# Two layers of linear attention and MLP, twice: passes, steps and small operations in another order

## The chip, the cores and the metric

The kernel runs on one core of a Trainium2 chip. The metric is the device time of one execution in microseconds (us); the time before is the median of three runs. A core has TensorE (PE in the profile, with PEld for its weight loads), VectorE (DVE), ScalarE (ACT), GpSimd (POOL) and SyncE (SP), each with its own queue of instructions that is worked in order. They wait for one another by semaphores. DMAs are issued from a queue and run beside the engines. Matrix products land in PSUM, which has eight banks of 128 x 512 f32 values; the other tiles lie in SBUF.

## The reference

x is 2048 rows of 512 values in bf16. Four layers follow one another, attention and MLP in turn, with the same weights in both rounds:

```
x = x + A(layernorm(x));  x = x + B(layernorm(x));  x = x + A(layernorm(x));  x = x + B(layernorm(x))
A: q, k, v = x @ wqkv, 32 heads of 16;  phi(t) = where(t > 0, t + 1, exp(t)) + 1e-6
   kv = sum over rows of phi(k) x v;  z = sum over rows of phi(k)
   out = (phi(q) @ kv) / (phi(q) . z + 1e-6), heads joined, @ wo
B: relu(x @ w1) @ w2, with w1 512 x 1376 and w2 1376 x 512
```

The layernorm subtracts the mean of a row's 512 values and divides by the root of their variance plus 1e-5. There is no softmax: attention is linear, so the sums over all rows (kv and z) must be complete before any output row can be made.

## The kernel before

The 2048 rows are 16 tiles of 128 rows, in four chunks of four tiles. All weights stay in SBUF; x stays there too, as `xin` (bf16) and `xres` (f32, the running sum).

The program is a graph of operations in Python (`g.add`, `add_flex`). Each names its engine, what it reads and writes by keys such as `("ps", b)` or `("big", unit)`, and a duration in ns (the constants `C_...` at the top). `_list_schedule` (from line 114) then simulates the machine: it repeatedly takes the operation that can start first, among the next `WINDOW` ones of each engine in the order in which they were added, gives PSUM tiles one of eight banks, lets an operation with alternatives (`add_flex`) choose its engine, and so writes down a fixed order for every engine's queue. `TAIL` is what it adds for a result to be seen. Semaphore waits are worked out from that order. So the order of `g.add` calls is only a priority, and a change in a cost, a key or a place can move instructions of the whole kernel.

The attention layer has these parts. `a_k` (four matmuls a tile) makes a tile's k; `phi_evac` takes it out of PSUM: ScalarE writes t + 1 (line 506) and exp(t) (508), VectorE clips the exp (510) and takes the larger (516). `a_q` does so for q, four groups of four matmuls a chunk. `a_z` sums phi(k) over rows with a column of ones. The value projection is not made for each row: `a_g` makes G = (normalised x)^T phi(k) in four PSUM banks, `a_g_evac` copies it, `a_kv` multiplies it with the v weights, and `a_m` masks the result to heads (line 582) and multiplies it with wo, giving `Mf` (589). `a_den` makes the denominators (matmuls with 32 columns), their log and its negative exp; `a_pqs` spreads the reciprocals over rows with 32-row matmuls (`Esel`) and scales phi(q) on VectorE (619). `a_fin` is four matmuls a tile of scaled phi(q) with Mf. `resid` (531 and 534) adds the result to x and sums each row; ScalarE's Square (540) sums the squares.

The MLP layer has `b_h` (ten column groups of 128, four chunks) with `b_relu` (641 and 642), `b_hl` for the last 96 columns in groups of 32, and `b_group` for the second product: for each of four groups of tiles, first the 32-row passes with the last 96 rows of w2 (`mk_small`, twelve matmuls that open four PSUM banks, or five in the very last group), then ten matmuls a tile for the other rows. A group `il` takes tile `il` of every chunk, so it needs the relu of all chunks.

The norm of a chunk, `ln_chunk`, is a chain of small operations on 128 x 4 values: mean, minus its square, variance, variance plus epsilon on VectorE (451, 453, 455, 457), the power -0.5 on GpSimd (459), and -mean times that (`nbias`) on VectorE (461). `ln_norm` then normalises a tile on ScalarE (470), VectorE (472) or GpSimd (475). The tiles are transposed by PE (494, evacuated by 498 or 499) for the first chunk or two of the first layer and for the first chunk of MLP layers, and by DMA (480) elsewhere. In the first layer the statistics come from `bn_stats` (439, 440) on VectorE; `ln_first(0)` treats tile 0 alone (708 to 714) and tiles 1 to 3 together.

All loads go out on SP's queue: tile 0 of x, tiles 1 to 3, the K weights, the Q weights, the other chunks of x, the V weights and the rest (lines 376 to 391). Sixteen matmuls on zeros (`WARM`, line 407) run while x is on its way. `layer_steps` gives the steps of a layer with what each needs; the loop behind it weaves the steps of the next layer in as soon as their chunk is there. In attention, `bar` is what follows the last k tile: z, denominators, G, kv, Mf and the last chunk of q; `p2(t)` is fin, norm and transposes of one chunk.

Of the kernel before, what the change touches and what calls it, by code (L numbers as in the profile page):

```python
# [31 lines left out]
C_POOL_POW = 1000.0  # L32
C_POOL_NORM = 900.0
C_SP_ISSUE = 60.0
TAIL = {PE: 70.0, ACT: 230.0, DVE: 80.0, POOL: 300.0, SP: 0.0}
SYNC_LAT = 40.0
LN_EXP_SET = 6
WINDOW = {PE: 64, ACT: 80, DVE: 80, POOL: 12, SP: 6}


class _Op:
    __slots__ = ("eng", "emit", "reads", "writes", "dur", "lat", "sdeps", "odeps", "idx",
                 "seq", "dma", "name", "t_start", "t_done", "issued", "pos", "nsucc", "alts")
# [19 lines left out]
class _Graph:  # L63

    def __init__(self):
        self.ops = []
        self.last_w = {}
        self.readers = {}
        self.tile_ops = {}
        self.ntiles = 0  # L70

# [5 lines left out]
    def add(self, eng, emit, reads=(), writes=(), dur=100.0, lat=0.0, dma=False, name=""):  # L77
        op = _Op(eng, emit, tuple(reads), tuple(writes), dur, lat, dma, name)
        op.idx = len(self.ops)
        deps = {}  # L80
# [36 lines left out]
def _list_schedule(ops, tile_ops, vbank, nbanks=8):  # L117
# [15 lines left out]
    pend = {e: [o for o in ops if e in engs_of(o)] for e in ENGINES}  # L133
# [4 lines left out]
    remaining = len(ops)  # L138

    def ready_time(o):  # L140
# [10 lines left out]
        if need:  # L151
            fr = sorted(x for x in bank_free if x is not None)
            if len(fr) < len(need):
                return None
# [5 lines left out]
    while remaining:  # L160
        best = None
        for e in ENGINES:
# [33 lines left out]
            if cand is not None and (best is None or cand[0] < best[0] - 1e-9  # L196
                                     or (abs(cand[0] - best[0]) <= 1e-9 and cand[1].idx < best[1].idx)):
# [46 lines left out]
def build_kernel(nc, A_x, A_wqkv, A_wo, B_w1, B_w2, out, n_layers_pairs=2, K_STT=0, Q_STT=0, A_PE_CHUNKS=1, windows=None,  # L244
                 WARM=16, SPLIT0=True, TAIL_SPLIT=True, LAST_HALVES=True, FIRST_PE_CHUNKS=2,
# [22 lines left out]
    with es:  # L268
# [32 lines left out]
        nm2 = sb("nm2", [128, NT], F32)  # L301
        var = sb("var", [128, NT], F32)
# [6 lines left out]
        veps0 = sb("veps0", [128, 1], F32)  # L309
        rstd0 = sb("rstd0", [128, 1], F32)  # L310
        nbias0 = sb("nbias0", [128, 1], F32)
# [28 lines left out]
        def dma(emit, reads, writes, xfer_ns, name):  # L340
# [5 lines left out]
            op = g.add(SP, _emit, reads, writes, dur=C_SP_ISSUE, lat=xfer_ns, dma=True, name=name)  # L346
# [23 lines left out]
        def h_keys(c):  # L370
            return [("big", il * RU + c) for il in range(4)]
# [3 lines left out]
        def ld_x(t, lo=0):  # L375
            dma(lambda e, t=t: e.dma_start(xin[:, 4 * t + lo:4 * t + 4, :], x_v[:, 4 * t + lo:4 * t + 4, :]),
                [], [("xin", i) for i in range(4 * t + lo, 4 * t + 4)], 1500.0 * (4 - lo) / 4.0, "ld_x%d" % t)
        dma(lambda e: e.dma_start(xin[:, 0, :], x_v[:, 0, :]), [], [("xin", 0)], 450.0, "ld_x0a")
# [4 lines left out]
        for t in range(1, NCH):  # L383
            ld_x(t)
# [590 lines left out]
```

## Time and profile before

| what | us |
|---|---|
| median of 3 runs (lowest, highest) | 293.84 (293.66, 294.12) |
| the profiled execution, its own time | 294.0 |
| its span in the profile | 292.3 |
| PE busy | 283.3 (97%) |
| DVE busy | 153.4 (52%) |
| ACT busy | 172.5 (59%) |
| POOL busy | 31.8 (11%) |
| first matmul on zeros; first on x (a transpose) | 1.23; 7.04 |
| first K product; first fin; first product of the MLP | 8.13; 59.16; 75.02 |
| first fin of the third layer; its MLP | 198.27; 214.13 |
| last matmul ends | 289.67 |

Busy is the sum of an engine's instructions, and the page's forty slices give its share of each fortieth of the span (7.3 us) in tenths. Matmuls overlap in the array, so their recorded lengths (380 ns for 512 columns) are longer than the distance between two starts; rates are read from starts. Some matmul records are missing. An engine that idles costs nothing unless another waits for it.

### The profile page before, as it was taken

The page shows a single profiled execution, that of the slowest core. Times are in us where ns is not written, and L with a number is a line of the kernel's source. Part 1 is how long each engine was busy: PE and PEld are TensorE (multiplying, and loading weights), DVE is VectorE, ACT ScalarE, POOL GpSimd, SP SyncE. Part 2 cuts the span into 40 slices and gives each one's busy share as a digit, 9 for nine tenths or more (in the row PEclk, how much of TensorE's full clock was granted, in tenths as well). Part 3 has the DMA queues.
Part 4 walks back from the last instruction along what each step waited for, and adds up shares of the span by engine and source line. Part 5 has one row for each costly group of instructions (what it writes and reads, how often), then busy time and mean ns, then how long its engine had stood idle before and what let it go on. Part 6 is the DMA issues. An engine that isn't in the chain of part 4 may idle for free.

```text
span 292.3 us, 4292 instructions
## 1 busy us (share of the span) xinstructions
PE 283.3 (97%) x1649; PEld 128.7 (44%) x1670; DVE 153.4 (52%) x438; ACT 172.5 (59%) x354; POOL 31.8 (11%) x42
## 2 busy tenths in 40 slices
PE   7899999999999999999999999999999999999996
PEld 3354444334444444444444443444444444444443
DVE  5899774999940000347464758928994000022223
ACT  2998596687866664335644899258786766300000
POOL 3102100002430000022020300000243000000000
PEclk9999999999999999999999999999999999999999
DMA  7995320000370000030303400000038000001222
GB/s 222 357 374 107 63 27 0 2 0 0 72 147 0 0 2 0 3 72 11 61 2 72 72 3 0 2 0 0 3 64 152 1 2 0 2 9 63 72 74 72
DMA packets 33780, 15.97 MB, mean 55 GB/s; under 512 B 25312, under 2 KB 33248, under 8 KB 33760
## 3 DMA queue, kind: packets, MB, share of 16 engines
q1 hardware_dynamic: 33760, 15.70, 21.8%
q8 instruction: 13, 0.21, 0.3%
q14 instruction: 7, 0.06, 0.1%
HBM read 7.31 MB, written 2.10 MB: 32 GB/s over the span
## 4 chain that ended last, share of the span: by engine, by line
PE 88%; DVE 6%; DMA 2%; ACT 2%; issue 1%; SPq 1%
PE ps L523 87%; DMA xin<-in_A_x_dram 2%; DVE big L619 2%; DVE xn L472 1%; DVE xres L534 1%; ACT Mf L589 1%; ACT big L506 1%; PE ps L494 0%; DVE bst L439 0%; DVE big L516 0%; DVE emscr L510 0%; ACT sqscr L540 0%; SPq L382 0%; ACT escr L508 0%; SPq L381 0%
## 5 line engine op out<-in xcount | busy, mean ns | idle before, releaser
L523 PE MATMUL ps<-Tb,w 128*128 128x512 bf16 (+1 forms) x416 | 75.0, 379 | 0.0
L523 PE MATMUL ps<-w,big 128*128 128x512 bf16 (+1 forms) x321 | 69.2, 372 | 1.3 <-issue 1.3
L641 ACT ACTIVATE big<-ps 128x512 bf16<-128x512 f32 x78 | 46.5, 596 | 19.6 <-PE ps L523 19.6
L523 PEld LDWEIGHTS ps<-Tb,w 128*128 128x128 bf16 (+1 forms) x416 | 33.5, 97 | 41.2 <-ACT big L641 1.7
L523 PEld LDWEIGHTS ps<-w,big 128*128 128x128 bf16 x330 | 31.4, 98 | 37.6 <-issue 2.3
L534 DVE SCALAR_TENSOR_TENSOR xres<-ps,xres 128x512 f32<-128x512 f32 x32 | 21.8, 687 | 47.2 <-PE ps L523 46.9
L540 ACT ACTIVATE sqscr<-xres 128x512 bf16<-128x512 f32 x48 | 29.9, 629 | 27.5 <-DVE xres L534 27.3
L506 ACT ACTIVATE big<-ps 128x512 bf16<-128x512 f32 x64 | 40.9, 643 | 7.6 <-PE ps L523 7.3
L508 ACT ACTIVATE escr<-ps 128x512 bf16<-128x512 f32 x64 | 41.3, 661 | 0.4 <-DVE emscr L510 0.4
L531 DVE TENSOR_TENSOR xin<-ps,xres 128x512 bf16<-128x512 f32 x15 | 10.4, 692 | 54.5 <-PE ps L523 54.5
L459 POOL TENSOR_TENSOR rstd<-veps,nhalf 128x4 f32<-128x4 f32 x15 | 16.1, 1072 | 175.9 <-DVE veps L457 155.8
L523 PE MATMUL ps<-Tb,wqkv 128*128 128x512 bf16 x128 | 30.6, 379 | 0.0
L523 PE MATMUL ps<-wqkv,Tb 128*128 128x512 bf16 x124 | 28.8, 379 | 1.5 <-ACT Tb L498 1.1
L523 PE MATMUL ps<-Mf,big 128*128 128x512 bf16 x126 | 28.9, 380 | 1.1 <-ACT Mf L589 0.8
L523 PE MATMUL ps<-big,xn 128*128 128x512 bf16 x124 | 29.7, 379 | 0.3
L516 DVE TENSOR_TENSOR big<-big,emscr 128x512 bf16<-128x512 bf16 x64 | 26.5, 422 | 1.2
L510 DVE TENSOR_SCALAR emscr<-escr 128x512 bf16<-128x512 bf16 x64 | 18.5, 296 | 12.3 <-ACT escr L508 12.1
L619 DVE TENSOR_TENSOR big<-big,ps 128x512 bf16<-128x512 bf16 x32 | 19.9, 680 | 1.3 <-PE ps L523 1.3
L523 PEld LDWEIGHTS ps<-wqkv,Tb 128*128 128x128 bf16 x128 | 12.1, 98 | 16.0 <-ACT Tb L498 1.5
L523 PEld LDWEIGHTS ps<-Mf,big 128*128 128x128 bf16 x128 | 11.9, 98 | 16.2 <-ACT Mf L589 1.3
L523 PEld LDWEIGHTS ps<-big,xn 128*128 128x128 bf16 x128 | 11.5, 97 | 13.1 <-issue 1.5
L523 PEld LDWEIGHTS ps<-Tb,wqkv 128*128 128x128 bf16 x128 | 11.5, 97 | 12.3 <-DVE big L619 0.4
(71 smaller groups left out, 184.6 us busy)
## 6 DMA issues: line engine op xcount, KB each, us to landing
wqkv<-in_A_wqkv_dram SPq DMA_DIRECT2D x3, 512.0 KB, 6.1
xin<-in_A_x_dram SPq DMA_DIRECT2D x3, 512.0 KB, 8.0
out_dram<-xin SPq DMA_DIRECT2D x3, 512.0 KB, 2.9
w<-in_B_w_dram SPq DMA_DIRECT2D x1, 1376.0 KB, 11.0
w<-in_B_w_dram SPq DMA_DIRECT2D x1, 1280.0 KB, 13.7
wo<-in_A_wo_dram SPq DMA_DIRECT2D x1, 512.0 KB, 8.8
xin<-in_A_x_dram SPq DMA_DIRECT2D x1, 384.0 KB, 3.3
w2l<-in_B_w_dram SPq DMA_DIRECT2D x4, 96.0 KB, 7.6
```

The costliest lines, as they stand in the source:

```text
L459: g.add(POOL, lambda e: e.tensor_tensor(rstd[:, sl], veps[:, sl], nhalf[:, 0:4], ALU.pow), [("veps", t), ("nhalf",)], [("rstd", t)], C_POO ...
L472: (DVE, lambda e: e.tensor_scalar(xn[:, i, :], src, rstd[:, i:i + 1], nbias[:, i:i + 1], ALU.mult, ALU.add), C_DVE_NORM_BF if first else 4 ...
L506: g.add(ACT, lambda e: e.activation(dst_ap, psv[:, b, :], ACTF.Identity, bias=1.0 + 1e-6, scale=1.0), [("ps", b)], [dst_key], C_ACT_PSUM, ...
L508: g.add(ACT, lambda e: e.activation(escr[:, s, :], psv[:, b, :], ACTF.Exp), [("ps", b)], [("escr", s)], C_ACT_EXP, name=name + "_exp")
L510: g.add(DVE, lambda e: e.tensor_scalar(emscr[:, s, :], escr[:, s, :], 1.0, 1e-6, ALU.min, ALU.add), [("escr", s)], [("emscr", s)], C_DVE_B ...
L516: g.add(DVE, lambda e: e.tensor_tensor(dst_ap, dst_ap, emscr[:, s, :], ALU.max), [dst_key, ("emscr", s)], [dst_key], 340.0, name=name + "_ ...
L523: last = e.matmul(o, l, r, start=st, stop=sp, skip_group_check=skip)
L531: g.add(DVE, lambda e: e.tensor_tensor(xin[:, i, :], psv[:, b, :], src, ALU.add), [("ps", b), skey], [("xin", i)], C_DVE_PSUM, name="resid ...
L534: g.add(DVE, lambda e: e.scalar_tensor_tensor(xres[:, i, :], psv[:, b, :], 0.0, src, ALU.add, ALU.add, accum_out=s1[:, si:si + 1]), [("ps" ...
L540: g.add(ACT, lambda e: e.activation(sqscr[:, q, :], xres[:, i, :], ACTF.Square, accum_out=s2[:, si:si + 1]), [("xres", i)], [("sqscr", q), ...
L619: g.add(DVE, lambda e, j=j, u=u: e.tensor_tensor(unit_ap(u), unit_ap(u), psv[:, bs[j], :], ALU.mult), [("ps", bs[j]), ("big", u)], [("big" ...
L641: g.add_flex([(ACT, lambda e: e.activation(h_evac_ap(c, t), pin(), ACTF.Relu), C_ACT_PSUM), (DVE, lambda e: e.tensor_scalar(h_evac_ap(c, t ...
```

## The change

- *32-row passes.* `b_group` is split into `b_small` (the 32-row passes of a group) and `b_main` (its other matmuls, for some of its tiles). The passes of group il + 1 are put between the third and the fourth tile of group il, and those of group 0 ahead of the last column group of the last `b_h`. The keys of the hidden values are kept for each chunk (`("big", unit, t)`) instead of for all.
- *Attention steps.* `bar` has another order: each chunk's denominator, spread and scaling stand between the parts of G; q of chunk 2 (first layer) or of chunks 0 to 2 (third layer) moves into it. Chunk 0's fin is written with Mf's part j outermost, as sixteen single matmuls into four banks (`a_fin4`). The last chunk's denominator moves from `bar` to `p2(0)`.
- *Ranks.* Operations of engines other than PE can carry an urgency (`g.urg`), which moves them forward in the scheduler's list by so many places: 300 for KVT and Mf, 100 for G's copies, 40 and 60 for chunk 0's second part and the last q. An operation that opens PSUM banks out of turn must leave one free (`RESERVE`).
- *Norm.* All the small steps of `ln_chunk` go to GpSimd, one more than before as the variance is taken in two; the norm of tiles 0 and 1 of a chunk runs on VectorE from mean and rstd, that of tiles 2 and 3 on VectorE or ScalarE; none on GpSimd.
- *First tiles.* Each of tiles 0 to 3 has its own chain with Ln and Exp on ScalarE in place of the power; later statistics wait for tile 3's norm; in the later chunks of the first layer tiles 0 to 2 are normalised on VectorE and tile 3 on ScalarE. The K weights are loaded from ScalarE's queue, x in pieces of 1, 1, 2 and 4 tiles ahead of the Q weights; `WARM` goes from 16 to 12.
- *Costs.* GpSimd's power is costed by its columns, its small steps at 150 ns, its tail at 60 ns instead of 300.

```diff
-C_POOL_POW = 1000.0
-C_POOL_NORM = 900.0
+C_POOL_POW0 = 420.0
+C_POOL_POW1 = 145.0
+C_POOL_SMALL = 150.0
...
+TAIL = {PE: 70.0, ACT: 230.0, DVE: 80.0, POOL: 60.0, SP: 0.0}
...
+RESERVE = 1
...
+        op.urg = self.urg if eng != PE else 0
...
+    def rank(o):
+        return o.idx - o.urg
+    ranked = sorted(ops, key=rank)
...
+            if o is not hd and len(fr) < len(need) + min(RESERVE, len(alloc_of[hd.idx])):
                 return None
...
         ld_x(0, 1)
-        dma(lambda e: e.dma_start(wqkv[:, :, D:2 * D], wq_v[:, :, D:2 * D]), [], [("wk",)], 1500.0, "ld_wk")
-        dma(lambda e: e.dma_start(wqkv[:, :, 0:D], wq_v[:, :, 0:D]), [], [("wq",)], 1500.0, "ld_wq")
-        for t in range(1, NCH):
-            ld_x(t)
+        ld_qk(D, "wk", ACT)
+        ld_x(1, 2)
+        ld_x(2, 4)
+        ld_x(4, 8)
+        ld_qk(0, "wq")
+        for t in range(2, NCH):
+            ld_x(4 * t, 4 * t + 4)
...
+            g.add(DVE, lambda e: e.bn_stats(bst[:, i, :], xin[:, i, :]), [("xin", i)] + ([("xn", 3)] if i > 3 else []),
+                  [("bst", i)], C_DVE_BNST, name="bnst%d" % i)
...
+        def ln_rstd_act(i):
+            g.add(ACT, lambda e: e.activation(veps[:, i:i + 1], mv[:, i, 1:2], ACTF.Ln, bias=EPS, scale=1.0),
+                  [("var", i)], [("veps", i)], 200.0, name="lnv%d" % i)
+            g.add(ACT, lambda e: e.activation(rstd[:, i:i + 1], veps[:, i:i + 1], ACTF.Exp, scale=-0.5),
+                  [("veps", i)], [("rstd", i)], 200.0, name="rstd%d" % i)
...
+            g.add(POOL, lambda e: e.tensor_scalar(mean[:, sl], s1[:, sl], -INV_D, None, ALU.mult),
+            g.add(POOL, lambda e: e.tensor_tensor(nm2[:, sl], mean[:, sl], mean[:, sl], ALU.mult),
+            g.add(POOL, lambda e: e.tensor_scalar(ex2[:, sl], s2[:, sl], INV_D, None, ALU.mult),
+            g.add(POOL, lambda e: e.tensor_tensor(var[:, sl], ex2[:, sl], nm2[:, sl], ALU.subtract),
+            g.add(POOL, lambda e: e.tensor_scalar(veps[:, sl], var[:, sl], 0.0, EPS, ALU.max, ALU.add),
             g.add(POOL, lambda e: e.tensor_tensor(rstd[:, sl], veps[:, sl], nhalf[:, 0:4], ALU.pow),
+            g.add(POOL, lambda e: e.tensor_tensor(nbias[:, sl], mean[:, sl], rstd[:, sl], ALU.mult),
...
+        def a_fin4(t, first_layer):
+            bs = [alloc_bank() for _ in range(4)]
+            for j in range(4):
+                u = pq_unit(j, t)
+                for il in range(4):
+                    mm_group(lambda j=j, il=il, u=u: [(psv[:, bs[il], :], big[:, u * 512 + 128 * il:u * 512 + 128 * il + 128], Mf[:, j, :],
+                                                       j == 0, j == 3, True)],
+                             bk(u) + [("Mf", j)], [("ps", bs[il])], C_MM512, "fin%d_%d" % (4 * t + il, j))
...
                 def o_step(il):
-                    b_group(il, last_layer)
+                    b_main(il, last_layer, 0, 3)
+                    if il < 3:
+                        b_small(il + 1, last_layer)
+                    b_main(il, last_layer, 3, 4)
...
+                def up_last():
+                    b_h(NCH - 1, range(NFULL - 1))
+                    b_small(0, last_layer)
+                    b_h(NCH - 1, range(NFULL - 1, NFULL))
```

The first layer's `bar` after the change:

```
                    if first_layer:
                        a_den(0)
                        g_rest(0)
                        a_den(1)
                        a_pqs(0)
                        g_rest(1)
                        a_kv(0, KB)
                        a_q(2)
                        a_pqs(1)
                        a_kv(1, KB)
                        g_rest(2)
                        a_den(2)
...
                    g_rest(3)
                    a_kv(2, KB)
                    a_pqs(2)
                    a_kv(3, KB)
                    a_m(KB)
                    g.urg = URG3
                    a_q(3)
                    g.urg = 0
```

## The prediction

> **What bounds the kernel now.** I read the page's busy lines and its forty slices first, then TensorE's list of waits, then the start in the timeline, and last the timeline of TensorE alone, looking for holes.
>
> ```profile
> PE 283.3 (97%) x1649; PEld 128.7 (44%) x1670; DVE 153.4 (52%) x438; ACT 172.5 (59%) x354; POOL 31.8 (11%) x42
> PE   7899999999999999999999999999999999999996
> DVE  5899774999940000347464758928994000022223
> ACT  2998596687866664335644899258786766300000
> ```
>
> TensorE (PE) is full from the third slice on at full clock. Everything else is a supplier. The change removes no matrix work, so it can only win holes in PE. These are the waits:
>
> ```profile
> PE ps L523 <- issue: 1.3, 8, 0.2
> PE ps L407 <- DVE wrm L400: 1.2, 1, 1.2
> PE ps L523 <- ACT Tb L498: 1.1, 2, 0.6
> PE ps L523 <- ACT Mf L589: 0.8, 1, 0.8
> PE ps L523 <- DVE big L516: 0.4, 1, 0.4
> ```
>
> Eight holes of "issue" (1.3 us in all) stand behind the 32-row passes; one waits for the evacuation of Mf, one for VectorE's phi, and the rest lie at the start:
>
> ```profile
> 2.96 0.69 DVE L439 BATCH_NORM_STATS2 bst<-xin 128x6 f32<-128x512 bf16 x1 [1.78 <-DMA xin<-in_A_x_dram]
> 4.14 0.56 POOL L710 TENSOR_TENSOR rstd<-veps,nhalf 128x1 f32<-128x1 f32 x1 [1.64 <-DVE veps L708]
> 4.53 1.29 DVE L439 BATCH_NORM_STATS2 bst<-xin 128x6 f32<-128x512 bf16 x2 [0.47 <-DMA xin<-in_A_x_dram]
> 6.38 0.14 DVE L712 SCALAR_TENSOR_TENSOR nbias<-mv,rstd 128x1 f32<-128x1 f32 x1
> 8.13 1.04 PE L523 MATMUL ps<-wqkv,Tb 128*128 128x512 bf16 x4 [0.63 <-ACT Tb L498]
> 9.85 1.29 DVE L439 BATCH_NORM_STATS2 bst<-xin 128x6 f32<-128x512 bf16 x2 [0.88 <-DMA xin<-in_A_x_dram]
> 10.34 3.07 PE L523 MATMUL ps<-wqkv,Tb 128*128 128x512 bf16 x12 [0.51 <-ACT Tb L498]
> 13.25 2.75 PE L523 MATMUL ps<-Tb,wqkv 128*128 128x512 bf16 x12
> ```
>
> Columns are start, length, instruction, count, idle time before. Tile 0's power is done at 4.70, yet its next step (nbias) starts at 6.38: VectorE is inside the statistics of tiles 1 to 3. K of tile 0 starts at 8.13, K of tile 1 at 10.34.
>
> ```profile
> 57.33 1.04 PE L523 MATMUL ps<-Tb,wqkv 128*128 128x512 bf16 x4
> 59.16 3.63 PE L523 MATMUL ps<-Mf,big 128*128 128x512 bf16 x16 [0.79 <-ACT Mf L589]
> 112.46 0.83 PE L523 MATMUL ps<-w2l,big 32*128 32x512 bf16 x12
> 113.44 8.58 PE L523 MATMUL ps<-w,big 128*128 128x512 bf16 x39 [0.16 <-issue]
> 121.95 0.83 PE L523 MATMUL ps<-w2l,big 32*128 32x512 bf16 x12
> ```
>
> The spacing of full matmuls is 0.2165 us (70.69 to 75.02 for 20). So four matmuls from 57.33 end their issue at 58.20, and the hole ahead of 59.16 is 0.96. Behind the 32-row pass 39 of 40 matmuls are on record. Forty take 8.66, and 121.95 minus 8.66 is 113.29: the missing record is the first, and the "issue" hole is an unrecorded matmul, not idleness.
>
> **The change part by part.** The sum is made against the profiled execution, 294.0 us (span 292.3 and 1.7 around it); the median shown is 0.16 below that.
>
> *32-row passes moved ahead of the last tile.* Twelve small matmuls from 112.46 to the first full one at about 113.23 take 0.77, of which 3 x 0.2165 is work (four run side by side) and 0.12 the two changes of shape. They are as many afterwards, elsewhere. Finer keys let a group start with only its own columns' relu, but no wait stands there today. 0; bounds -0.2 and +0.4 (two changes more of some 0.1 at each of two places). They take four PSUM banks (five in the last group) while the previous group holds its last; VectorE, which frees them, is idle there (1.47 us ahead of each residual in the last group).
>
> *First tiles' chains apart.* x of tile 0 lands at 2.96 today. The K weights now go out on ScalarE's queue at the same time; 384 KB more of x landed 1.57 later (4.53), so 128 KB cost about 0.5 and shared traffic may cost tile 0 between 0 and 0.5: I take 0.2, 3.16. Statistics 0.69, aggregate 0.18, then Ln and Exp on ScalarE, each priced by the one small ACTIVATE (0.20), with 0.05 between: 4.6. Norm 0.38: 5.0. The warm-up, four matmuls shorter, ends near 5.7 (nine at 0.427 until 5.02, then three at 0.22), so the transposes start at 5.7, their evacuation (0.60) ends at 6.75 and K0 starts there: 1.4 earlier. VectorE spends 0.66 + 0.17 + 0.38 = 1.2 a tile, so tile 3 is normalised near 8.7; transposes 0.3, evacuation 0.6 and one K in front put its K at 10.2 and Q at 11.1 rather than 13.25: -2.1. On SP's queue x4-7 is now fourth instead of fifth: at 0.4 to 0.5 an issue it goes out near 2.2 instead of 2.77, and Q's weights behind it. Those come behind the same 2 MB as x4-7 did, which landed at 9.8; enough. ScalarE's DMA issue (0.4 to 0.5 by SP's rows) delays its table load, 1.04 to 2.32 today, well ahead of 4.1. Next in line are tiles 4 to 7: their statistics wait for tile 3's norm by the new dependency, 8.7 instead of 9.85, which is 1.15 earlier only; from there to the norms it is 5.64 today, so 14.4, against Q's end at 14.56. Just covered, and first z and G passes (0.54 and 1.89) are there to fill. -2.1; bounds -1.1 (that chain sets it) and -3.0.
>
> *Attention steps, fin by j.* Sixteen single matmuls with Mf j outermost need only Mf 0 at first: its copy ends at 57.65, ahead of 58.20; later copies come every 0.48 and a block of four takes 0.87. The 0.96 goes; bounds 0 (four banks are needed at once) and -0.96: -0.9. In the third layer no such hole exists (nothing). The phi wait at 164.99 (0.41) and the shorter one ahead of it (some 0.2) come from VectorE's norms in front of phi, one stretched to 0.99 beside GpSimd's norms. Norms leave GpSimd, but order is new: -0.3, bounds -0.6 and +0.6. The denominators, twelve matmuls in one go (47.34 to 48.11, 0.77), become three of 0.33 each (62.72 to 63.05): +0.22, and +0.06 in the third layer, where there are two goes (0.55 and 0.38): +0.3, bounds 0 and +0.6.
> The page TensorEngine Tiling of the Trainium skill (Key Properties) says that a change of tiling mode drains the TensorE, which speaks against more separate goes. It gives no time; where the rows give 0.1 a change, the rule alone would put the sum higher by an unknown amount.
>
> *Norm's small steps on GpSimd.* Five VectorE steps of 0.16 leave each of twelve chunks (9.6 busy); thirteen GpSimd norms (0.95) go to VectorE (0.55, 7.2 at most) or ScalarE (0.81). That balances; GpSimd's own queue then holds only these chains, one chunk behind the other, and no norm in front of the next chain. GpSimd's six small steps a chunk are in no row: 0.10 (its memset of 128x4) and 0.56 (a power of one column) bound one; I take 0.2, nearer the memset because nothing in them is a power. After the last square the chain is then 3 x 0.2 + 1.01 + 0.2 = 1.8; today it is 3.1 (64.74 to 67.82), with two waits for VectorE in it. Its cover is large: chunk 1's transpose is issued at 76.70 and lands 4.3 later, while its first use is 40 matmuls after 75.02, at 83.7: 2.7 of slack. 0; if the cover went, the excess would be paid: bounds 0 and +5.8 (rival two).
> GPSIMD Engine Reference of the Trainium skill (Key points) states that GpSimd shares its SBUF interfaces with VectorE and that they contend. The row agrees: the power took 1.01 typically and 1.65 beside VectorE's bf16 work. Were each of seven steps stretched by the same 0.64, a chunk would take 4.5 longer, beyond the slack.
>
> *Urgency ranks, a reserved bank, other costs* redraw the static order everywhere. Today's order leaves 0.96 + 0.6 = 1.6 of holes behind the start; a new one may leave 0 to 1.6 of its own. I take 0.7, a little under the middle. ScalarE gets eight small steps and three norms (4.0), and has 4.15 idle ahead of 32.84: nothing.
>
> Sum: -2.1 - 0.9 - 0.3 + 0.3 + 0.7 = -2.3; 294.0 gives 291.7, the median 291.5. The case's own range is 289.4 to 293.2.
>
> **The rivals.** *The start's gain is caught by tiles 4 to 7.* For it: VectorE is busy 6.50 of 6.50 us between 11.5 and 18, and it is what makes the next tiles. Then -1.1 at the start, -0.5 at Mf, and +0.3 + 0.7: -0.6, 293.2. Against it: z and G passes can fill.
> *Slower: VectorE held by GpSimd.* Its queue is in order, and a norm that waits for a GpSimd chain holds the residuals that free PSUM. Place: the two stretches where it is full,
>
> ```profile
> 59.20:75.00 15.80, 15.65 (x87) 7.17 (x89) 15.17 (x53) 13.06 (x35) 2.79 (x3) 1.00 0.00 1
> ```
>
> (third bracketed group: VectorE, 15.17 of 15.80). Two chunks of each attention layer fall there. At 0.56 a step, four chunks x four steps x 0.36 above my price is 5.8: 293.84 - 2.3 + 5.8 = 297.3. It decides from 2.3 on, a step of 0.34. Against it: GpSimd's memset takes 0.10.
> *No change.* The new order leaves holes for all it wins (2.3), as where Q of chunk 2 enters the stretch 46.5 to 59.2: ScalarE's 9.52 plus 4 x 0.96 is 13.4, against PE's 12.7 + 3.5 = 16.2. It fits, if evenly spread. 293.8.
>
> **How the numbers follow.** Forecast 0.60, caught start 0.15, GpSimd 0.17, no change 0.08. A measurement tells about 0.2% (0.6 us) from nothing, so the first and nearly all of the second count as faster, some of the edges as the same or slower: 0.70, 0.12, 0.18. The range runs from 289.3, the best sum I believe, to 295.0, some way towards GpSimd's case, leaving out about 0.1 on either side.
>
> **What would show it.** K of tile 0 near 6.8 and Q near 11 in the timeline; no wait for Mf; the same 0.77 for 32-row passes in a new place; GpSimd's small steps near 0.2; PE's last end some 2.3 earlier with the 2.6 us of drain behind it unchanged. Wrong it would be made by PE waits for VectorE's residual between 57 and 73, or by holes between 11 and 16.

## The result and the profile after

The changed kernel takes 293.15 us (median of six, 292.64 to 293.48) against 293.92 for the kernel before (median of six, 293.66 to 294.12): a ratio of 0.9972 with a 95% interval of 0.9959 to 0.9985. It is faster by 0.8 us, a third of the 2.3 that was forecast. The profiled execution took 293.29 with a span of 291.5. Two later series gave 0.9951 (0.9935 to 0.9966) and 0.9957 (0.9944 to 0.997): the changed kernel took the same there (293.10 and 293.02), the kernel before 294.49 and 294.31, so that the gain was 1.4 and 1.3. Why the kernel before took longer in them stays open; only its execution of 294.0 was profiled.

The page after, its busy lines and slices as they were shown of before:

```profile
PE 285.5 (98%) x1666; PEld 128.7 (44%) x1666; DVE 144.9 (50%) x381; ACT 177.5 (61%) x368; POOL 36.7 (13%) x99
PE   7899999999999999999999999999999999999996
DVE  3999565999920000246453737849993000022223
ACT  3899497859886664246565878657988766300000
```

VectorE lost 8.5 us of work (153.4 to 144.9), ScalarE took 5.0 and GpSimd 4.9 more. TensorE is as full as before: the first and the last slice, where it is not, look the same. Its list of waits is shorter:

```profile
PE ps L428 <- DVE wrm L421: 1.2, 1, 1.2
PE ps L562 <- ACT Tb L537: 0.8, 2, 0.6
PE ps L533 <- DVE xn L510: 0.4, 1, 0.4
PE ps L562 <- ACT escr L547: 0.3, 1, 0.3
PE ps L562 <- ACT Mf L631: 0.3, 1, 0.3
```

The wait of 0.8 for Mf is now 0.3, and VectorE's phi (0.4) has left the list. ScalarE's exp (`escr`) is new in it; the wait for VectorE's normalised tile (`xn`) stood at 0.3 in the list before. The eight "issue" waits are gone as well; the prediction read the one it followed up as an unrecorded matmul, and in the trace after all forty matmuls between two sets of 32-row passes are on record, in the same time.

The clearest account is that of the stretches between first starts on TensorE, taken from the timelines of both kernels:

| stretch, us | before | after | difference |
|---|---|---|---|
| start to the first Q product | 13.25 | 12.95 | -0.30 |
| first Q to first fin | 45.91 | 45.91 | 0.00 |
| fin stage of the first layer (first fin to first MLP product) | 15.86 | 15.61 | -0.25 |
| MLP and third layer up to its first fin | 123.25 | 123.36 | +0.11 |
| fin stage of the third layer | 15.86 | 15.57 | -0.29 |
| last MLP, to the end of the last matmul | 75.53 | 75.53 | 0.00 |

The sum is -0.73, and the drain behind it stayed at 2.6. So the start was to bring 2.1 and brought 0.3, and the holes inside the attention layer were refilled by others. The start in the timeline of the changed kernel (start, length, instruction, count, idle before):

```profile
3.44 0.69 DVE L460 BATCH_NORM_STATS2 bst<-xin 128x6 f32<-128x512 bf16 x1 [2.27 <-DMA xin<-in_A_x_dram]
...
6.05 1.44 DVE L460 BATCH_NORM_STATS2 bst<-xin 128x6 f32<-128x512 bf16 x2 [0.78 <-DMA xin<-in_A_x_dram]
...
1.24 5.19 PE L428 MATMUL ps<-wrm 128*128 128x512 bf16 x12 [1.24 <-DVE wrm L421]
6.26 0.39 PE L533 MATMUL ps<-ident,xn 128*128 128x128 bf16 x4
...
7.34 1.04 PE L562 MATMUL ps<-wqkv,Tb 128*128 128x512 bf16 x4 [0.63 <-ACT Tb L537]
8.78 0.87 PE L533 MATMUL ps<-ident,xn 128*128 128x128 bf16 x8 [0.40 <-DVE xn L510]
9.86 1.04 PE L562 MATMUL ps<-wqkv,Tb 128*128 128x512 bf16 x4 [0.21 <-ACT Tb L537]
```

The statistics of tile 0 wait for its x until 3.44 instead of 2.96, those of tile 1 until 6.05 instead of 4.53. The warm-up of twelve matmuls ran cold almost to its end, so the transposes of tile 0 start at 6.26. K of tile 0 starts 0.8 earlier than before, K of tile 1 only 0.5 (9.86 for 10.34), and Q 0.3.

Where Mf is made, the hole ahead of the first fin is gone and another stands four matmuls earlier:

```profile
57.02 1.08 ACT L631 ACTIVATE Mf<-ps 128x512 bf16<-128x512 f32 x2
57.24 0.69 DVE L632 CAST Mf<-ps 128x512 bf16<-128x512 f32 x1
57.67 0.39 PE L562 MATMUL ps<-wo,KVT 128*128 128x512 bf16 x1 [0.26 <-ACT Mf L631]
...
57.99 1.04 PE L562 MATMUL ps<-Tb,wqkv 128*128 128x512 bf16 x4
58.10 0.69 DVE L632 CAST Mf<-ps 128x512 bf16<-128x512 f32 x1
...
58.86 1.46 PE L562 MATMUL ps<-Mf,big 128*128 128x512 bf16 x6
```

From 57.99 four matmuls at 0.2165 reach 58.86, where fin starts with no idle time. But the fourth matmul that makes Mf starts 0.64 behind the third, 0.42 late, because it waits for a bank that ScalarE's first Mf copy must free.

### The profile page after: what moved, and what is told of

Read it like the earlier page. It is cut to its first block, busy times and chain, and to the rows that moved or that the text cites. A ratio compares the mean times of both kernels' runs of the same rounds, so it can differ in the third digit from the quotient of the medians.

```text
span 291.5 us, 4312 instructions
## 1 busy us (share of the span) xinstructions
PE 285.5 (98%) x1666; PEld 128.7 (44%) x1666; DVE 144.9 (50%) x381; ACT 177.5 (61%) x368; POOL 36.7 (13%) x99
## 3 DMA queue, kind: packets, MB, share of 16 engines
q1 hardware_dynamic: 33248, 15.17, 21.3%
## 4 chain that ended last, share of the span: by engine, by line
PE 93%; ACT 3%; DMA 2%; DVE 1%; SPq 0%; issue 0%
PE ps L562 92%; DMA xin<-in_A_x_dram 2%; ACT big L545 1%; PE ps L533 1%; ACT escr L547 1%; DVE bst L460 0%; ACT Tb L537 0%; SPq L392 0%; ACT xn L515 0%; ACT Mf L631 0%; DVE xin L744 0%; ACT veps L473 0%; DVE mv L462 0%; ACT rstd L475 0%
## 5 line engine op out<-in xcount | busy, mean ns | idle before, releaser
L562 PE MATMUL ps<-w,big 128*128 128x512 bf16 (+1 forms) x330 | 71.1, 373 | 0.0
L695 ACT ACTIVATE big<-ps 128x512 bf16<-128x512 f32 x79 | 46.1, 595 | 19.5 <-PE ps L562 19.4
L545 ACT ACTIVATE big<-ps 128x512 bf16<-128x512 f32 x64 | 39.9, 627 | 10.7 <-PE ps L562 10.6
L573 DVE SCALAR_TENSOR_TENSOR xres<-ps,xres 128x512 f32<-128x512 f32 x32 | 21.1, 688 | 49.6 <-PE ps L562 49.6
L547 ACT ACTIVATE escr<-ps 128x512 bf16<-128x512 f32 x64 | 39.6, 634 | 0.0
L562 PE MATMUL ps<-wqkv,Tb 128*128 128x512 bf16 x128 | 30.6, 380 | 1.4 <-ACT Tb L537 0.8
L562 PE MATMUL ps<-big,xn 128*128 128x512 bf16 x128 | 30.4, 379 | 0.0
L562 PE MATMUL ps<-Mf,big 128*128 128x512 bf16 x128 | 29.5, 379 | 0.0
L662 DVE TENSOR_TENSOR big<-big,ps 128x512 bf16<-128x512 bf16 x32 | 20.5, 680 | 6.8 <-PE ps L562 6.7
L482 POOL TENSOR_SCALAR mean<-s 128x4 f32<-128x4 f32 x12 | 3.1, 258 | 149.6 <-DVE xres L573 149.2
L499 DVE TENSOR_SCALAR xn<-xres,mean,rstd 128x512 bf16<-128x512 f32 x33 | 16.6, 541 | 3.6 <-POOL rstd L492 3.5
```

Of the source, the lines that this page charges most:

```text
L482: g.add(POOL, lambda e: e.tensor_scalar(mean[:, sl], s1[:, sl], -INV_D, None, ALU.mult), [("s1", i) for i in tl], [("mean", i) for i in tl ...
L499: alts = [(DVE, lambda e: e.tensor_scalar(xn[:, i, :], xres[:, k, :], mean[:, i:i + 1], rstd[:, i:i + 1], ALU.add, ALU.mult), 460.0)]
L545: g.add(ACT, lambda e: e.activation(dst_ap, psv[:, b, :], ACTF.Identity, bias=1.0 + 1e-6, scale=1.0), [("ps", b)], dst_keys, C_ACT_PSUM, n ...
L547: g.add(ACT, lambda e: e.activation(escr[:, s, :], psv[:, b, :], ACTF.Exp), [("ps", b)], [("escr", s)], C_ACT_EXP, name=name + "_exp")
L562: last = e.matmul(o, l, r, start=st, stop=sp, skip_group_check=skip)
L573: g.add(DVE, lambda e: e.scalar_tensor_tensor(xres[:, i, :], psv[:, b, :], 0.0, src, ALU.add, ALU.add, accum_out=s1[:, si:si + 1]), [("ps" ...
```

## The experiments

"The control" below is the changed kernel itself, measured on the same chip as what it is compared with: 293.10 (292.79 to 293.29) on the chip of all experiments but the last two runs (the second of three series there, in which the kernel before took 294.37, 294.49 and 294.56), 293.02 on theirs. Except where it is said, the order that the planner wrote for every engine is kept, and only the named instructions are moved in it. In the diffs `move(name, queue, place)` stands for taking one operation out of its engine's list and putting it in at that place.

### What the shared traffic alone costs

The kernel before, with only its load of the K weights sent from ScalarE's queue:

```
 # kernel before
+move("ld_wk", ACT, first)
```

> The kernel before, with only the K weights moved to ScalarE's queue as its first instruction, orders kept: the disputed cost by itself. Theory A: statistics of tile 0 near 3.4 instead of 2.96, tiles 1 to 3 near 5.8 instead of 4.53, K of tile 1 near 11.3 instead of 10.34, and the time 0.5 to 1.2 above before. Theory B: landings may move, K of tile 1 within 0.3 of 10.34, time the same.

It took 296.32 (295.12 to 297.81), ratio to before 1.0065 (1.004 to 1.009). In its start the x of tiles 1 to 3 is late:

```profile
2.97 0.70 DVE L439 BATCH_NORM_STATS2 bst<-xin 128x6 f32<-128x512 bf16 x1 [1.79 <-DMA xin<-in_A_x_dram]
...
6.91 1.29 DVE L439 BATCH_NORM_STATS2 bst<-xin 128x6 f32<-128x512 bf16 x2 [2.84 <-DMA xin<-in_A_x_dram]
```

It lands 2.4 later than in the kernel before (6.91 for 4.53), K of tile 0 moves from 8.13 to 10.51, and in the profiled execution, of 295.69, the last matmul ends 1.65 later. Moving this load takes the transfers off no resource: it only lets the weights compete with x. The page DMA: Bandwidth & Descriptors of the Trainium skill (section "Issuing engines are not separate DMA queues") says just that, that transfers from several engines interleave on the same 16 DMA engines and only the issue time is saved; the 6.91 agrees.

### The load back in SP's queue

```
+move("ld_wk", SP, 4th: behind the three first loads of x)
```

> The changed kernel with one DMA moved: the K weights go out on SP's queue again, fourth, behind x of tiles 0 to 3; every engine's order of instructions is kept. Theory A (the start's gain was lost because the K weights share the DMA engines with x): statistics of tile 0 start near 2.96 us instead of 3.44 and those of tiles 1 to 3 by 4.6 instead of 6.05; K of tile 0 stays near 7.3, behind the warm-up; K of tile 1 follows at once, near 8.4 instead of 9.86; Q starts at 11.0 to 11.6 instead of 12.95; the time falls by 0.8 to 1.6 against the changed kernel (291.6 to 292.4). Theory B (the chain over VectorE and ScalarE is what holds the tiles): statistics move, but Q still starts after 12.5 and the time stays at 293.1.

292.91 (292.25 to 293.29), 0.9944 (0.9928 to 0.996): not distinguishable from the control. x does land early, at 2.94 and 4.68, but in the profiled execution, the slowest of the six, nothing comes of it:

```profile
6.33 0.63 PE L533 MATMUL ps<-ident,xn 128*128 128x128 bf16 x4
...
7.66 1.04 PE L562 MATMUL ps<-wqkv,Tb 128*128 128x512 bf16 x4 [0.58 <-ACT Tb L537]
...
8.73 0.60 ACT L545 ACTIVATE big<-ps 128x512 bf16<-128x512 f32 x1 [0.48 <-PE ps L562]
...
9.22 0.59 ACT L537 ACTIVATE Tb<-ps 128x512 bf16<-128x512 bf16 x1
...
9.87 1.04 PE L562 MATMUL ps<-wqkv,Tb 128*128 128x512 bf16 x4 [0.71 <-ACT Tb L537]
...
12.96 0.81 PE L562 MATMUL ps<-Tb,wqkv 128*128 128x512 bf16 x3
```

TensorE is in its cold warm-up until 6.33, so K of tile 0 starts at 7.66. ScalarE's queue is in order, and in it t + 1 of tile 0 (line 545, which needs K of tile 0) stands ahead of the evacuation of tile 1's transposes. It runs at 8.73, the evacuation at 9.22, and K of tile 1 can start at 9.87. So K of tile 1 follows K of tile 0 by 2.2, whatever x does. By this trace alone the shared traffic costs nothing; the next run shows that this is only because a second bound of the same size stands behind it.

### The load back, and a shorter warm-up

```
+move("ld_wk", SP, 4th)
-                for k in range(WARM):      # 12
+                for k in range(8):
```

> As the run before, with 8 matmuls on zeros instead of 12, orders kept. If the warm-up is what K of tile 0 waits for, its transposes start near 5.2 instead of 6.26 and K near 6.3; if the clock has risen by then, the time is 0.3 to 0.9 below the run before. If the clock has not risen, the first K matmuls stand 0.427 apart, and the time is the same or up to 0.5 above it. Under theory B no change.

292.54 (292.19 to 293.37), 0.9942 (0.9925 to 0.996). Q starts at 11.92 instead of 12.96, and 1.0 us is kept to the last matmul in the profiled execution:

```profile
6.63 1.02 PE L562 MATMUL ps<-wqkv,Tb 128*128 128x512 bf16 x4 [1.28 <-DMA wqkv<-in_A_wqkv_dram]
...
8.84 1.04 PE L562 MATMUL ps<-wqkv,Tb 128*128 128x512 bf16 x4 [0.73 <-ACT Tb L537]
...
11.92 1.24 PE L562 MATMUL ps<-Tb,wqkv 128*128 128x512 bf16 x5
```

Now the K weights themselves are waited for (1.28), and K of tile 1 still follows by 2.2. Two of the six times lie near 293.3 and the others near 292.4; only one of the latter was profiled.

### The shorter warm-up alone

The changed kernel with `range(8)` and the K weights still on ScalarE's queue. The control was run beside it.

> The changed kernel with 8 matmuls on zeros instead of 12, all orders kept, K weights still from ScalarE's queue. Theory C (the end of the warm-up and ScalarE's queue, which puts the evacuation of tile 0's transposes ahead of Ln of tile 1 and the copy of K 0 ahead of the evacuation of tile 1, pass the start on in lockstep): transposes of tile 0 start near 5.3 (norm of tile 0 ends 5.27) instead of 6.26, K of tile 0 near 6.4, Q near 12.0, the span 0.7 to 1.1 shorter. The rival (the late landing of x binds after all, as tiles 1 to 3 have their statistics at 6.05): K of tile 1 stays above 9.5 and the span falls by less than 0.4.

> The changed kernel unaltered, on the same chip as the three runs beside it: its ratio to before should repeat, 0.996 to 0.9985; the others are compared with it.

293.54 (292.8 to 295.41 in twelve runs), 0.9978 (0.9957 to 0.9998); the control 293.10, 0.9951 (0.9935 to 0.9966). The shorter warm-up saves nothing: x of tile 1 arrives at 6.03, and TensorE waits for its normalised tile until 8.77. In the profiled execution (294.07, granted clock 0.994) the matmuls behind that hole run at half the rate:

```profile
6.51 1.04 PE L562 MATMUL ps<-wqkv,Tb 128*128 128x512 bf16 x4 [0.63 <-ACT Tb L537]
8.77 1.09 PE L533 MATMUL ps<-ident,xn 128*128 128x128 bf16 x8 [1.22 <-DVE xn L510]
9.86 1.89 PE L562 MATMUL ps<-wqkv,Tb 128*128 128x512 bf16 x4
```

Four matmuls take 1.89 at 9.86, for 1.04 at 6.51: they start 0.427 apart again instead of 0.2165.

The control of the last pair shows the hold of x from the other side, with no edit at all. In its profiled execution the clock rose earlier, and K of tile 0 started at 6.49, 0.85 ahead of the first profile of the same kernel:

```profile
6.49 1.04 PE L562 MATMUL ps<-wqkv,Tb 128*128 128x512 bf16 x4 [0.63 <-ACT Tb L537]
8.62 0.87 PE L533 MATMUL ps<-ident,xn 128*128 128x128 bf16 x8 [1.09 <-DVE xn L510]
9.71 1.04 PE L562 MATMUL ps<-wqkv,Tb 128*128 128x512 bf16 x4 [0.21 <-ACT Tb L537]
```

K of tile 1 gained 0.15 of the 0.85 (9.71 for 9.86), as its normalised tile came late behind x (statistics at 5.88).

So two suppliers meet at K of tile 1. With this order of ScalarE's queue it starts in the traces some 3.82 behind the first statistics of tile 1 or some 2.2 behind K of tile 0, whichever is later:

| profiled execution | statistics of tile 1 | K of tile 0 | K of tile 1 | behind the statistics | behind K of tile 0 |
|---|---|---|---|---|---|
| before | 4.53 | 8.13 | 10.34 | 5.81 | 2.21 |
| changed | 6.05 | 7.34 | 9.86 | 3.81 | 2.52 |
| changed, first control | 5.81 | 7.66 | 9.87 | 4.06 | 2.21 |
| changed, control of the last pair | 5.88 | 6.49 | 9.71 | 3.83 | 3.22 |
| eight warm-up matmuls | 6.03 | 6.51 | 9.86 | 3.83 | 3.35 |
| load on SP's queue | 4.68 | 7.66 | 9.87 | 5.19 | 2.21 |
| load on SP's queue, eight | 4.65 | 6.63 | 8.84 | 4.19 | 2.21 |

Q follows K of tile 1 by 3.1 in all of them but the one with the low clock and the kernel before (2.9). With the load moved alone a late K of tile 0 held K of tile 1, with the warm-up cut alone a late x; with both, Q came 1.0 earlier. In these executions each hid the other. The medians are less sharp: against the control the load alone stands at -0.2, the warm-up alone at +0.4, both at -0.6, and the load alone has one time of 292.25, near the lowest with both (292.19). K of tile 0 varies from 6.33 to 7.66 among the traces with twelve warm-up matmuls, and an early one would explain that time; that execution was not profiled.

### Another order of the first tiles

Eight warm-up matmuls, the K weights third on SP's queue, and the first tiles' small operations put in another order on ScalarE and VectorE:

```
+move("ld_wk", SP, behind tile 1's x)
+ACT: lnv1 and rstd1 directly behind rstd0; lnv2, rstd2, trev1 behind trev0; lnv3, rstd3 behind k0_lin
+DVE: bnag1 behind bnst1; norm1, bnag2 behind bnst2; norm2, bnag3 behind bnst3; esel behind trev2
```

> 8 matmuls on zeros; K weights third on SP's queue, behind x of tiles 0 and 1; in ScalarE's and VectorE's queues the steps of tiles 1 to 3 moved ahead of what waits for TensorE (Ln and Exp of tile 1 ahead of the evacuation of tile 0, evacuation of tile 1 ahead of the copy of K 0, the small copy for the spread behind). Theory C: K of tile 0 near 6.0, K of tile 1 near 7.2 instead of 9.86, Q near 11.0 instead of 12.95; if all of it is carried, the time falls 1.7 to 2.2 below the changed kernel. The rival, as the prediction's first one: tiles 4 to 7 are not ready and K of tile 4 comes no earlier than 16.7 (17.69 in the changed kernel), so it falls by 1.0 at most.

293.52 (292.96 to 295.64 in twelve runs), 0.9975 (0.9957 to 0.9993). In the profiled execution, one of its fastest, Q starts at 12.06, but K of tile 4 only at 17.35:

```profile
12.06 3.62 PE L562 MATMUL ps<-Tb,wqkv 128*128 128x512 bf16 x16
16.07 1.04 PE L533 MATMUL ps<-ident,xn 128*128 128x128 bf16 x12 [0.39 <-DVE xn L510]
...
17.35 1.02 PE L562 MATMUL ps<-wqkv,Tb 128*128 128x512 bf16 x4
```

From Q to K of tile 4 it takes 5.29, in the changed kernel 4.74: 0.55 of the gain is given back to tiles 4 to 7, the prediction's first rival. As a way to a faster start this failed. Nor does it test ScalarE's order by itself: the evacuation of tile 1 stands ahead of t + 1 here, but on VectorE the norm of tile 1 (7.26) stands behind the statistics of tile 2, whose x came at 6.65, and K of tile 1 (8.96) still follows K of tile 0 (6.61) by 2.35.

### Filling the holes of the start

As the load back with eight warm-up matmuls, and in the first two holes three matmuls on zeros each, which keep TensorE busy:

```
+three matmuls ps[:, 0, :] <- wrm behind the transpose that follows those of tile 0
+three matmuls ps[:, 0, :] <- wrm behind the transposes of tile 2
```

> A candidate to beat both: the changed kernel with K weights fourth on SP's queue, 8 matmuls on zeros ahead, and three more on zeros behind tile 0's transposes and three behind those of tiles 1 and 2, into a PSUM bank that nothing holds then, so that the holes of 1.3 and 0.7 us there are filled; all orders kept. If the spread of the runs with 8 (292.2 to 293.4 us) comes from the clock falling in those holes, the extra matmuls hold it: Q near 11.9 as in the best run with 8, span 290.5, every run within 0.4 of 292.3, and the time 0.7 to 1.0 below the changed kernel on this chip (293.1). If the spread comes from elsewhere it stays, and the median is near 292.6.

292.50 (292.25 to 292.69), 0.9932 (0.9913 to 0.9951). The median is that of the run without filling, but of its six times none lies near 293.3. That fits a clock which no longer drops; as the slower executions were not profiled, it is not shown.

### Fin tile by tile

The forecast gave the end of the Mf hole to fin's new order, j outermost. Here the sixteen single matmuls of each attention layer are put back tile by tile:

```
-fin0_0, fin1_0, fin2_0, fin3_0, fin0_1, ...
+fin0_0, fin0_1, fin0_2, fin0_3, fin1_0, ...
```

> The changed kernel with the sixteen matmuls of chunk 0's fin in the order of before (tile by tile, Mf parts inside), banks and all other orders kept. As the prediction had it, the j order is what removes the hole ahead of fin: up to 0.9 of idle comes back behind the first three matmuls in the first layer, and the time rises by 0.5 to 0.9. The rival: Mf's copies are now shared by ScalarE and VectorE and the last ends at 58.79 in the changed kernel, before a fourth matmul at 59.5 needs it, so the j order does nothing: same time within 0.2.

293.05 (292.9 to 293.23), 0.9955 (0.9941 to 0.9969): the control's time, and no hole ahead of fin either:

```profile
57.62 1.04 PE L562 MATMUL ps<-Tb,wqkv 128*128 128x512 bf16 x4
58.49 1.67 PE L562 MATMUL ps<-Mf,big 128*128 128x512 bf16 x7
```

So beside the shared copies the order of j is worth nothing. What differs from before and is left are these copies: four on ScalarE, 57.05 to 59.11, before; two on ScalarE and two on VectorE, done at 58.79, after. With four ScalarE copies the last would land near 59.1, later than fin tile by tile needs it; with j outermost it would still be in time. The kernel with the shared copies taken back was not run, so this half is argued from the rows, and j outermost may do alone what the copies do.

### The norm of tile 15

In the changed kernel ScalarE normalises tile 15 at 33.87 for 0.80, in front of an exp for which K of chunk 2 waits; TensorE loses 0.31 ahead of 35.22. Here that norm is VectorE's:

```
+move("norm15", DVE, behind nbias15), as xin minus mean times rstd
```

> The changed kernel with one instruction moved: the norm of tile 15 in the first layer, which the change fixes to ScalarE, runs on VectorE behind the last nbias there; all else kept. If this norm (0.80 at 33.87) in front of the exp is what holds the PSUM bank for the last K of chunk 2 (0.31 of idle ahead of 35.22), the hole goes and first fin comes 0.3 earlier relative to Q's start: 45.6 instead of 45.91 between them. The rival: the bank was late anyway, the distance stays at 45.9.

292.72 (292.48 to 292.85), 0.9939 (0.9921 to 0.9958), 0.4 below the control. From Q to fin it takes 45.56 instead of 45.91, and the sixteen K matmuls run through:

```profile
32.15 3.62 PE L562 MATMUL ps<-wqkv,Tb 128*128 128x512 bf16 x16
...
33.30 0.41 DVE L954 TENSOR_SCALAR xn<-xin,mv,rstd 128x512 bf16<-128x512 bf16 x1
33.70 0.59 ACT L547 ACTIVATE escr<-ps 128x512 bf16<-128x512 f32 x1
```

So this hole is a cost of the change's own placement of the norm, and part of what swallowed the gain at Mf.

### The 32-row passes back

```
-b_small(il + 1) ahead of the last tile of group il
+b_small(il) at the start of group il
```

> The changed kernel with the eight 32-row passes back where they stood before, right ahead of their own group's first full matmul; all else kept. As the prediction costed the move at nothing: from the MLP's first product to its end the same 75.5 (fourth layer) within 0.2, and the time within 0.3. If the move hides a switch or a relu wait, up to 0.2 at each of eight places comes back, 0.5 to 1.6 in all.

293.17 (293.02 to 293.39), 0.9954 (0.9937 to 0.997), against 293.10: nothing, as forecast. In the changed kernel each set of passes takes 0.75 to 0.76 to the next full matmul, wherever it stands:

```profile
111.04 0.82 PE L562 MATMUL ps<-w2l,big 32*128 32x512 bf16 x12
...
119.25 0.83 PE L562 MATMUL ps<-w2l,big 32*128 32x512 bf16 x12
120.00 8.81 PE L562 MATMUL ps<-w,big 128*128 128x512 bf16 x40
```

### GpSimd's small steps doubled

Each of the six small steps of a chunk's norm is done twice, the first time into a tile that nobody reads:

```
-e.tensor_tensor(nm2, mean, mean, mult)
+e.tensor_tensor(unused, mean, mean, mult); e.tensor_tensor(nm2, mean, mean, mult)
...
```

> The changed kernel with each of the six small GpSimd steps of a chunk done twice, once into an unused tile, all orders kept: some 0.3 more a step, so a chunk's chain grows by 1.2 behind the last square and GpSimd's busy time by 16 to 20. If the chain has the cover that the prediction gave it (2.7 of slack), the time rises by 0.3 at most; if VectorE's queue is held by it where that is full (the second rival), up to four chunks pay 1.2 each and the time rises by 1 to 5.

294.95 (294.62 to 295.17), 1.0011 (0.9995 to 1.0027): 1.85 above the control. The fin stage takes 16.17 for 15.61, MLP and third layer 124.34 for 123.36, the second fin stage 15.87 for 15.57. VectorE's busy time stays (145.0 for 144.9), so its own work was not slowed. New in TensorE's waits are these:

```profile
PE ps L569 <- DVE big L562: 0.4, 1, 0.4
...
PE ps L540 <- ACT xn L510: 0.3, 1, 0.3
...
PE ps L569 <- DMA Tb<-xn: 0.2, 1, 0.2
```

They are waits for phi, for a normalised tile and for a DMA transpose. GpSimd's busy time grows by 13.4 (36.7 to 50.1), 1.1 a chunk, so the 2.7 of slack that the prediction read at one chunk's transpose would have hidden it. It did not: the chain has little cover.

### The small steps on VectorE

First as the source has it before, with the steps' engine in `ln_chunk` set to VectorE and all orders drawn anew by the planner:

```
-            g.add(POOL, lambda e: e.tensor_scalar(mean[:, sl], s1[:, sl], -INV_D, None, ALU.mult),
+            g.add(DVE, lambda e: e.tensor_scalar(mean[:, sl], s1[:, sl], -INV_D, None, ALU.mult),
...
```

> The changed kernel with the small steps of ln_chunk on VectorE again (four fused steps of 0.16 ahead of the power and one behind it), norms as in the changed kernel; the scheduler makes a new order, so small differences mean little. If the chain on GpSimd has too little cover (doubling its steps cost 1.9), the shorter one saves part of the third layer's holes (0.48 ahead of 171.56, 0.2 ahead of 162.97): 0.3 to 0.7 less. If VectorE's queue is the tighter place, its 9.6 of extra work in the stretches of fin, where it is full, costs 0.3 to 1.5.

294.77 (294.54 to 295.15), 1.001 (0.9997 to 1.0022): 1.67 above the control. Fin stages of 16.14 and 15.98, and 0.62 more between them, where K of the third layer waits 0.66 for a DMA transpose. As engine and order change together here, the second run moves the steps alone, into VectorE's queue at the places which the written times give them:

```
+move(mean, nm2, ex2, var, veps, nbias of every chunk, DVE, by their times)
```

> The changed kernel with every engine's order kept, only the six small steps of each chunk's norm put into VectorE's queue at the place that the written order's times give them (72 instructions; the power stays on GpSimd). Theory one, the place of the small steps is what the 1.67 us of the kernel with these steps on VectorE came from: the fin stages grow by 0.3 to 0.6 each (15.6 to about 16.0) and the third layer by 0.3 or more, the whole is 1.0 to 2.0 above the control, near 294.5. Theory two, it came from the order being drawn anew: the whole is within 0.4 of the control, about 293.1 to 293.5, and the stages keep 15.6 and 123.4.

294.82 (294.56 to 295.08), 1.002 (1.0011 to 1.0029), against 293.02 for the control beside it: 1.80 more. The two fin stages take 16.83 and 16.24, 1.2 and 0.7 more, and the stretch between them 0.2 less. The windows of the first fin stage (the bracketed groups are TensorE, its weight loads, VectorE, ScalarE, GpSimd), the control first:

```profile
58.70:74.31 15.61, 15.61 (x90) 7.18 (x88) 15.61 (x42) 11.99 (x31) 4.84 (x14) 1.00 0.01 3
```

```profile
58.78:75.61 16.83, 15.98 (x90) 7.21 (x88) 16.65 (x54) 12.15 (x30) 2.02 (x2) 1.00 0.01 1
```

VectorE is busy for the whole stage in the control, in which TensorE is full too. Twelve small steps more on it make the stage 1.22 longer, and TensorE waits 0.9 for the scaled phi (`big`, line 662), which those steps delayed. So the 1.7 to 1.8 is the place of the steps, in the order of this kernel, and not the drawing of a new order.

### The two gains together

The filled start and the norm of tile 15 on VectorE in one kernel:

```
+the start of the filled kernel
+move("norm15", DVE, behind nbias15)
```

> The changed kernel with K weights fourth on SP's queue, eight warm-up matmuls and six filling ones behind the transposes of tiles 0 and 2, and with the norm of tile 15 on VectorE. If the two gains lie in different places they add: the start 0.6 and the hole ahead of K of chunk 2 0.35, so 0.9 to 1.0 below the control, about 292.1. If the start's order gives back what the norm frees (tile 4's chain is on VectorE too), 0.6 or less.

> The changed kernel itself, as the control on the same chip: 293.1, with its fin stages 15.6 each and its third layer 123.4 from the first product of the MLP to the third layer's first fin.

292.15 (291.99 to 292.25), 0.9929 (0.9915 to 0.9942), with the control at 293.02 (292.81 to 293.2), 0.9957 (0.9944 to 0.997). 0.87 below the changed kernel: nearly the sum of 0.60 and 0.38 that the parts gave against their control. It is the fastest kernel of this study. Its start:

```profile
6.70 1.02 PE L562 MATMUL ps<-wqkv,Tb 128*128 128x512 bf16 x4 [0.85 <-DMA wqkv<-in_A_wqkv_dram]
...
8.90 1.04 PE L562 MATMUL ps<-wqkv,Tb 128*128 128x512 bf16 x4
...
11.99 1.67 PE L562 MATMUL ps<-Tb,wqkv 128*128 128x512 bf16 x7
```

## Why the prediction was right and wrong

**Sign and bounds.** Faster came true, at 293.15 inside 289.3 to 295.0. The size did not: -0.8 for -2.3 (-1.4 and -1.3 in the later series).

**First tiles, -2.1: measured -0.30. This is the step that failed.** Three parts of it were wrong. "Shared traffic may cost tile 0 between 0 and 0.5: I take 0.2" looked at tile 0 alone. It paid 0.48 (0.02 in the control of the last pair, so the bounds held), but tile 1, which the estimate did not charge at all, paid 1.52. "The warm-up ends near 5.7" took the clock's rise of the one trace of before (5.02) for a fixed time; in the trace after all twelve matmuls were cold and it ended at 6.3, in another execution of the same kernel at 5.4. And "VectorE spends 1.2 a tile, so tile 3 is normalised near 8.7" followed VectorE's work only. ScalarE's queue puts the t + 1 of tile 0 between tile 0's evacuation and tile 1's, so that K of tile 1 follows K of tile 0 by 2.2 even where x is early and the warm-up short. In the trace after, x holds it longest (9.86), and K of tile 0 would not have let it start before 9.55. The two late suppliers are of about the same size: in the profiled executions undoing one brought Q nothing, undoing both 1.0 (11.92, with K of tile 0 at 6.63, near the 6.75 of the forecast); 0.6 of it shows in the median. The 0.8 that is left to the 11.1 of the forecast lies, by the rows, in ScalarE's order, which no run moved by itself.

**The first rival** named 293.2 and the loss of the start's gain, but by the wrong hand. Tiles 4 to 7 did not catch it: from Q to K of tile 4 it takes 4.74, as in the kernel before (4.78, where the first of the sixteen matmuls, at 18.03 by the spacing, is not on record). Only with the other order of the first tiles did that mechanism show, for 0.55.

**Mf, -0.9: the hole went, the reason given was not needed, and the stretch gained nothing.** Fin tile by tile has no hole either, so beside the shared copies, which the prediction did not foresee, j outermost earns 0; alone it was not run. In the same stretch the change lost 0.42 ahead of the fourth Mf matmul and 0.31 ahead of K of chunk 2, the second shown by moving one norm. Of the rest, 0.23, the denominators explain 0.11: their twelve matmuls go in two parts of 0.54 and 0.34 there, for one of 0.77 before. The other 0.12 was not found.

**Own holes, +0.7; phi -0.3; denominators +0.3.** The holes that can be named in the trace after are 0.42 and 0.31 in the first layer, 0.48 (ahead of 171.56, behind exp on ScalarE) and 0.20 (ahead of 162.97) in the third: 1.4, twice what was taken and inside the 0 to 1.6. The stretch with phi and the third layer's denominators came out 0.11 longer in all; its terms can't be told apart.

**Norm on GpSimd, 0: the term was put together wrongly.** The price of a step was near: 0.20 to 0.27 for 0.2, though the steps start 0.3 apart, and the chain behind the last square takes 2.4 (159.23 to 161.61) rather than 1.8. But "2.7 of slack", read at one chunk, is not the cover of the chain: doubled steps cost 1.85. And taking the steps from VectorE, costed at nothing, is worth 1.7 in this kernel's order, since the fin stages, with VectorE at 15.17 of 15.80, were where it could bind. The fin stages gained 0.25 and 0.29 on before, and TensorE now has no idle time in the first of them. The second rival did not come true; its point, 0.34 a step, was not reached. With doubled steps 0.86 of the 1.85 fell in the two stretches that it named, but the waits on record are for normalised tiles and phi, not for PSUM banks, and its own sum, 16 steps with 0.19 more each, would have made 3.0.

**32-row passes, 0:** right, also in the 0.76 a set.

**No change:** its argument, that the new order leaves holes for what it wins, holds for the stretch from Q to fin (0.00), not for the whole.

## What to carry to other kernels

Where several late suppliers meet, find each one's own time at the point where they meet: an experiment that removes one and shows nothing has not cleared it until the others are removed too. Price a start by the slowest engine queue in order, operation by operation, and charge a moved load to all transfers that it now runs beside. And work taken from an engine that is full in one stage is priced in that stage, whatever its share of the span is.

## What the runs showed of the hardware

- The clock's rise differs between executions. The matmuls on zeros, twelve or sixteen from 1.24 on, started 0.427 apart until somewhere between 4.6 and 6.3: until 4.6 in one execution of the changed kernel and until 6.3 in another. The page TensorE: Matmul & The Clock Gate of the Trainium skill (Part 1) lays a spread of 0.5 us to either side to a free-running window of 3.4 us; the spread here is wider, 1.7 between these two, and the window itself is seen in no trace.
- A clock once risen dropped after holes of 0.45, 0.63 and 1.22 between short bursts (5.28 to 9.86 with eight warm-up matmuls), and five spacings of 0.43 instead of 0.22 followed, 1.0 in all. In the control of the last pair, with twelve, holes of 0.63 and 1.09 (6.49 and 8.62) were followed by no such drop; what decides is not shown.
- GpSimd's operations on 128 x 4 values take 0.20 to 0.27 each and start 0.3 apart; the same on VectorE takes 0.15 to 0.17.
